# A gated recurrence feeding an MLP on one core: another hand-written order of steps, products of the state in two halves, and two 64-byte gaps in the memory map

## The chip, the core and the metric

One core of one Trainium2 chip. The metric is the device time of one execution in microseconds, the median over runs. All inputs lie in the chip's memory before the execution starts, and the output of 384 x 3072 float32 is written back to it.

## The reference, cut

```python
# q, k, v, alpha: (4, 8, 768, 48); w_in: (384, 2048); w_out: (2048, 384)
for t in range(S):
    state = alpha[:, :, t, :, None] * state + einsum('bhd,bhde->...', k[:, :, t], v[:, :, t])   # an outer product
    y[:, :, t] = einsum('bhd,bhde->bhe', q[:, :, t], state)
x = y.transpose(0, 2, 1, 3).reshape(3072, 384)
h = x @ w_in
sp = maximum(h, 0) + log1p(exp(-abs(h)))
return (h * erf(sp)) @ w_out
```

A recurrence over 768 steps for 32 heads of 48 channels (the attention part), and behind it an MLP from 384 to 2048 and back to 384, in float32 precision.

## The kernel before, in words

**Chunks.** The 768 steps are cut into 12 chunks of 64. A chunk's attention is written as matrix products: decays are accumulated by a scan (`a1`), keys and queries are scaled by them (`a2`, `a3`), `s` multiplies keys by queries (64 products, line 293), `t` transposes the keys (8 products, line 309), `u` adds the chunk to the running state T (64 products, line 326, then VectorE), `q` multiplies queries by the old state and `y` multiplies the masked scores by the values (128 products each, line 362), both into the same accumulator `py`. A chunk gives 256 tokens of x, and each chunk has its own MLP (`Moe`).

**MLP.** x is split into a high and a low part (`x_hi`, `x_lo`), the weights too (`wi_hi`, `wi_lo`, `wo_hi`, `wo_lo`), and three products hi*hi, hi*lo, lo*hi stand for one of full precision. The 2048 hidden channels of a chunk go in 4 groups of two halves: `H` multiplies by w_in (18 products of 128x256 a half, line 443), `U`, `L1`, `L2`, `G`, `Z` make the gated value on ScalarE and VectorE, and `O` splits it into `gh` and `gl` and multiplies by w_out (18 products of 128x256 a half, line 509). These are 3456 "big" products in all; the attention makes 4504 "small" ones. A product is two instructions of TensorE's stream, a weight load (PEld) and a matmul (PE).

**Weights.** They arrive as 8-byte floats in 28 pieces (`wi_0` to `wi_11`, `wo_0` to `wo_15`) and are turned into a high and a low float32 part by some six operations of ScalarE and VectorE each. The first group of H needs wi_0, wi_1 and wi_2.

**Order.** Every step is a Python generator that yields after each piece of work. `SCHED` is one long text of step names, written out by hand or by a program that is not part of the kernel; `steps()` takes the names one after another, and each name lets its step run on to its next yield (`v:` in front puts a copy on VectorE in place of ScalarE). TensorE, ScalarE, VectorE and the queue of SyncE keep exactly this order, so the text sets what each engine does next; semaphores do the waiting. Behind a `q` a memset of `token` on GpSimd is made to wait for it, and the first instruction of that chunk's `y` waits for the token.

**Memory.** `tile_pool`s are laid out one behind the other: constants and weights, then `at` (T), `xp` (x_hi and x_lo, two of each), `big` (23 buffers of 4160 bytes), `gp` (gh, gl and the output tile, two of each).

Of the kernel before, what the change touches and what calls it, by code (L numbers as in the profile page):

```python
# [30 lines left out]
la_0 a1_0 a2_0 a2_0 a2_0 la_2 a1_2 la_1 a1_1 lq_0 a3_0 wi_5 wi_5 a2_0 v:wi_5 lk_0 wi_5 a2_0 a2_1 a2_1 wi_1 wi_5 wi_0  # L31
a2_0 a2_1 wi_0 v:wi_0 lv_0 t_0 lk_1 a2_1 wi_5 wi_0 a2_1 a2_2 s_0 a2_2 s_0 s_0 y_0 a2_1 wi_2 wi_1 a2_2 wi_0 v:wi_1 wi_1
t_0 t_0 t_1 lq_1 a3_1 wi_2 v:wi_2 u_0 t_1 s_1 wi_1 wi_4 wi_4 u_0 s_1 wi_3 t_1 wi_1 v:wi_4 lv_1 wi_2 s_1 wi_2 q_1 wi_3
wi_0 wi_0 y_1 wi_7 v:wi_3 u_1 wi_2 wi_4 wi_2 wo_13 y_0 wi_1 y_0 H_0_0_0 H_0_0_1 wi_6 y_1 wi_8 wi_7 v:wi_7 wi_11 wi_4
y_1 y_1 wo_13 wi_10 wi_3 y_0 v:wo_13 wi_4 y_0 H_0_0_0 lk_2 wi_3 wi_6 wo_13 v:wi_6 wi_3 wi_7 wi_5 wi_9 H_0_0_0 wi_6
wi_4 wo_10 wi_8 wi_3 v:wi_8 H_0_0_1 H_1_0_0 H_1_0_1 H_0_0_1 U_0_0 u_1 wi_10 a2_2 H_1_1_0 wo_3 L1_0_0 H_0_1_0 H_0_1_0
y_1 wo_2 wi_9 wi_8 H_0_1_0 wi_6 wi_8 v:wi_9 H_1_1_1 H_1_0_1 lq_2 H_1_0_0 a2_2 wi_8 wo_10 v:wi_10 wi_6 wi_7 wi_7 wi_8
wo_0 wi_9 la_3 wo_3 wi_11 H_1_1_0 H_1_1_0 H_1_1_1 lv_2 v:wi_11 H_0_1_1 wi_6 v:wo_3 wi_7 H_0_2_1 a2_2 wo_13 t_2 L1_0_0
wo_13 a3_2 H_0_1_1 H_1_1_1 H_0_2_1 wi_9 H_1_0_1 H_0_1_1 H_0_2_0 wo_13 wi_9 s_2 wo_0 wi_11 wi_10 H_1_0_0 v:wo_10 v:wo_0
wo_2 wi_11 q_2 wi_9 t_2 H_0_2_0 H_1_2_0 v:wo_2 H_0_2_1 wi_10 a1_3 t_2 u_2 wo_1 wo_14 s_2 s_2 y_2 wi_11 H_0_2_0 wo_3  # L40
wi_10 wi_10 a2_3 wo_1 wo_9 v:wo_1 wo_2 wo_10 H_1_2_0 wi_11 lq_3 L1_0_0 a2_3 H_0_3_0 wo_9 H_0_3_1 u_2 v:wo_9 wo_14
v:wo_14 L2_0_0 a2_3 G_0_0 wo_10 wo_2 wo_2 wo_3 L2_0_0 H_1_2_0 lk_3 H_1_2_1 wo_14 a2_3 H_0_3_1 wo_2 H_0_3_0 a2_3 wo_14
H_1_3_0 U_0_1 y_2 y_2 y_2 a3_3 H_1_2_1 y_2 H_0_3_0 wo_5 lv_3 a2_3 L1_0_1 wo_3 wo_3 wo_6 H_0_3_1 wo_10 Z_0_0 H_1_3_1
wo_14 wo_14 wo_1 H_2_2_1 H_1_3_1 H_1_3_1 H_1_3_0 H_1_3_0 wo_6 v:wo_6 H_2_1_1 t_3 Z_0_0 H_1_2_1 wo_4 s_3 q_3 wo_5 t_3
t_3 u_3 v:wo_5 L1_0_1 O_0_0_1 L1_0_1 wo_9 s_3 s_3 wo_6 wo_1 wo_0 y_3 O_0_0_0 y_3 U_0_3 wo_5 u_3 wo_0 wo_4 O_0_0_0
wo_11 v:wo_1 L2_0_1 O_0_0_1 H_2_0_1 H_2_0_0 y_3 wo_1 H_2_1_0 y_3 wo_12 U_0_2 G_0_1 wo_9 y_3 H_2_2_0 wo_0 wo_0 H_2_0_0
v:wo_4 wo_4 L2_0_1 wo_7 wo_4 Z_0_1 L1_0_2 H_3_2_0 wo_9 L1_0_2 wo_10 H_2_2_0 H_2_2_0 wo_8 wo_6 H_2_0_0 H_2_2_1 H_3_3_1
wo_7 wo_7 H_2_0_1 L1_0_3 wo_15 Z_0_1 wo_12 wo_12 wo_7 v:wo_6 wo_4 v:wo_11 H_2_0_1 wo_7 O_0_0_0 H_3_3_1 wo_8 O_0_0_0
L1_0_2 O_0_1_0 wo_9 wo_4 L2_0_2 H_2_1_0 v:wo_8 H_3_3_1 H_3_0_0 L1_0_3 wo_5 wo_7 L1_0_3 L2_0_2 H_2_1_1 H_2_1_0 wo_6
v:wo_5 H_3_3_0 wo_7 wo_5 wo_8 wo_12 v:wo_11 wo_11 O_0_1_0 wo_8 wo_11 G_0_2 L2_0_3 O_0_0_1 H_3_0_1 H_2_2_1 lq_4 H_3_3_0  # L50
# [729 lines left out]
```

## Time and profile before

| | |
|---|---|
| median of 3 runs | 563.23 us (559.36 to 564.34) |
| the profiled execution | 559.77 us, of which the span from first to last instruction is 558.0 us |
| TensorE matmuls busy | 498.1 us (89%) |
| VectorE busy | 481.1 us (86%) |
| ScalarE busy | 474.2 us (85%) |
| mean granted clock of TensorE | 0.964 of full speed |
| moved by DMA | 43.8 MB |

How to read it: the busy time of TensorE counts every moment in which at least one product is in flight, so it does not tell how fast products follow each other. Idle time with the releaser "issue" is time in which an engine had no semaphore left to wait for in the profile and still did not start its next instruction. q8 is the DMA queue that carries TensorE's instructions.

### The profile page before, as it was taken

Reading aid. Unit: us, or ns where it says so; the run is one execution under the profiler, and the core shown is the slowest. Engines: PE = TensorE matmul, PEld = TensorE weight load, DVE = VectorE, ACT = ScalarE, POOL = GpSimd, SP = SyncE. Lnnn points to the kernel's source line nnn. Section 1 sums busy time; section 2 is a strip of 40 time slices with the busy share of each in tenths; the row PEclk is TensorE's granted clock in tenths of the full one; section 3 lists DMA queues with packets and bytes.
Section 4 is the critical chain, followed back from the end, with each engine's and each line's share of the span. In section 5 each row is a group of like instructions: output and inputs, shape, how many; then the busy total and the mean of one; then the engine's idle time right before and its main releaser. Section 6 shows DMA issues by size and latency. Waiting matters only on the chain.

```text
span 558.0 us, 17772 instructions
## 1 busy us (share of the span) xinstructions
PE 498.1 (89%) x7962; PEld 486.9 (87%) x7962; DVE 481.1 (86%) x583; ACT 474.2 (85%) x626; POOL 4.2 (1%) x25
## 2 busy tenths in 40 slices
PE   0659979799999989799799799989899998999994
PEld 0549979799999989799799799979899998999994
DVE  6858796889999998899799699988899998999892
ACT  5836996889999989799889798897899899798870
POOL 2000000000000000000000000000000000000000
PEclk9958979899999999999999799999999999999997
DMA  8874152212132141202102210221012200000001
GB/s 333 300 257 163 45 187 95 92 55 77 39 127 95 40 146 38 80 2 86 60 1 105 80 39 21 86 79 51 20 41 67 75 3 12 20 2 29 29 2 62
DMA packets 16019, 43.78 MB, mean 78 GB/s; under 512 B 1600, under 2 KB 6208, under 8 KB 15936
## 3 DMA queue, kind: packets, MB, share of 16 engines
q1 hardware_dynamic: 15936, 42.57, 21.9%
q8 instruction: 64, 1.05, 0.8%
q14 instruction: 19, 0.16, 0.1%
HBM read 37.85 MB, written 4.72 MB: 76 GB/s over the span
## 4 chain that ended last, share of the span: by engine, by line
PE 89%; issue 7%; DVE 2%; DMA 1%; POOL 0%; DVEq 0%
PE ph L443 38%; PE acc L509 37%; PE py L362 7%; PE pu L326 3%; PE pS L293 3%; PE pn L309 2%; DVE A L258 1%; DMA A<-in_alpha_dram 1%; DVE Q L281 0%; DVE K L276 0%; DVE rw L271 0%; DVE sT L300 0%; DVE o L210 0%; DVE wbuf L559 0%; DVE wbuf L555 0%
## 5 line engine op out<-in xcount | busy, mean ns | idle before, releaser
L443 PE MATMUL ph<-x_hi,wi_hi 128*128 128x256 f32 x576 | 145.5, 289 | 0.0
L443 PE MATMUL ph<-x_hi,wi_lo 128*128 128x256 f32 x576 | 144.5, 288 | 0.0
L509 PE MATMUL acc<-gh,wo_hi 128*128 128x256 f32 x576 | 139.7, 280 | 0.6 <-issue 0.6
L509 PE MATMUL acc<-gh,wo_lo 128*128 128x256 f32 x576 | 139.0, 279 | 0.0
L443 PEld LDWEIGHTS ph<-x_hi,wi_hi 128*128 128x128 f32 x576 | 112.5, 195 | 0.7 <-issue 0.3
L443 PEld LDWEIGHTS ph<-x_hi,wi_lo 128*128 128x128 f32 x576 | 112.4, 195 | 0.0
L509 PEld LDWEIGHTS acc<-gh,wo_hi 128*128 128x128 f32 x576 | 108.0, 188 | 1.1 <-issue 0.8
L509 PEld LDWEIGHTS acc<-gh,wo_lo 128*128 128x128 f32 x576 | 108.1, 188 | 0.0
L200 ACT ACTIVATE s<-s 128x1024 f32<-128x1024 f32 x96 | 100.5, 1056 | 4.3 <-DVE t L473 3.9
L443 PE MATMUL ph<-x_lo,wi_hi 128*128 128x256 f32 x576 | 82.5, 284 | 3.0 <-issue 3.0
L509 PE MATMUL acc<-gl,wo_hi 128*128 128x256 f32 x576 | 80.9, 280 | 0.0
L443 PEld LDWEIGHTS ph<-x_lo,wi_hi 128*128 128x128 f32 x576 | 74.7, 191 | 3.5 <-issue 3.2
L497 DVE TENSOR_TENSOR gl<-hs,gh 128x512 fp32r<-128x512 f32 x96 | 65.0, 685 | 12.2 <-PE acc L509 9.1
L509 PEld LDWEIGHTS acc<-gl,wo_hi 128*128 128x128 f32 x576 | 73.3, 188 | 0.2
L206 ACT ACTIVATE hs<-ph 128x512 f32<-128x512 f32 x88 | 50.6, 591 | 20.2 <-PE ph L443 20.1
L473 DVE TENSOR_TENSOR t<-s,w 128x1024 f32<-128x1024 f32 x48 | 58.1, 1218 | 1.8 <-ACT w L200 1.5
L199 ACT ACT_TABLE_LOAD x46 | 59.0, 1283 | 0.8
L484 DVE TENSOR_TENSOR s<-s,w 128x1024 f32<-128x1024 f32 x48 | 57.9, 1218 | 1.4 <-ACT s L200 1.0
L475 DVE SCALAR_TENSOR_TENSOR w<-t,w 128x1024 f32<-128x1024 f32 x48 | 58.3, 1217 | 0.2
L486 DVE SCALAR_TENSOR_TENSOR hs<-s,hs 128x1024 f32<-128x1024 f32 x48 | 58.2, 1217 | 0.1
L200 ACT ACTIVATE w<-w 128x1024 f32<-128x1024 f32 x48 | 50.4, 1055 | 0.4
L200 ACT ACTIVATE w<-s 128x1024 f32<-128x1024 f32 x48 | 50.0, 1056 | 0.3
(66 smaller groups left out, 581.6 us busy)
## 6 DMA issues: line engine op xcount, KB each, us to landing
A<-in_alpha_dram SPq DMA_DIRECT2D x12, 520.0 KB, 4.1
Q<-in_qk_dram SPq DMA_DIRECT2D x12, 512.0 KB, 3.5
wst<-in_moe_w_in_dram SPq DMA_DIRECT2D x12, 512.0 KB, 7.1
K<-in_qk_dram SPq DMA_DIRECT2D x12, 512.0 KB, 3.5
raw_v<-in_v_dram SPq DMA_DIRECT2D x12, 512.0 KB, 3.2
wst<-in_moe_w_out_dram SPq DMA_DIRECT2D x16, 384.0 KB, 3.6
out_dram<-o SPq DMA_DIRECT2D x12, 256.0 KB, 2.2
out_dram<-o SPq DMA_DIRECT2D x12, 128.0 KB, 1.7
```

The lines of the kernel that those rows point to most:

```text
L199: nc.scalar.preload_act_table_set(table)
L200: nc.scalar.activation(*args, **kw)
L206: nc.scalar.activation(out, in_, AF.Copy, scale=scale)
L293: nc.tensor.matmul(out=ps[half][i * TC : (i + 1) * TC, m * NP + pair, :], lhsT=K[rows, m, pair, i, :], rhs=Q[rows, m, pair, i, :], start=T ...
L362: nc.tensor.matmul(out=self.py[i][c0 : c0 + 32, kt, m, :], lhsT=left[r0 : r0 + rows, l0 : l0 + 32], rhs=right[r0 : r0 + rows], start=kt == ...
L443: nc.tensor.matmul(out=ph[:, u * self.TB : (u + 1) * self.TB], lhsT=wt[:, kt, fs], rhs=xt[:, kt, : self.TB], start=k == 0 and u == 0 and k ...
L473: nc.vector.tensor_tensor(out=t, in0=s, in1=w, op=ALU.mult)
L475: nc.vector.scalar_tensor_tensor(out=w, in0=t, scalar=2.0, in1=w, op0=ALU.add, op1=ALU.mult)
L484: nc.vector.tensor_tensor(out=s, in0=s, in1=w, op=ALU.mult)
L486: nc.vector.scalar_tensor_tensor(out=h, in0=s, scalar=RT2 / 2, in1=h, op0=ALU.subtract, op1=ALU.mult)
L497: nc.vector.tensor_tensor(out=gl, in0=gg, in1=gh.bitcast(F32), op=ALU.subtract)
L509: nc.tensor.matmul(out=self.acc[dm // n][:, dm % n * self.TB : (dm % n + 1) * self.TB], lhsT=wt[:, f, dm * P : (dm + 1) * P], rhs=gt[:, u ...
```

## The change

It has three parts.

1. `terms()` loops over the batch half m outside and yields after each m, so that `q` and `y` each become two pieces of 64 products; `q` now has 2 names in `SCHED` and `y` 6 (5 before).
2. `SCHED` is another text. The same 7960 products, loads and elementwise operations are issued, in another order.
3. Two tiles of 16 float32 (64 bytes a partition) that nothing uses, `shift_x` behind T and `shift_g` behind `big`. `xp` and `big` begin 64 bytes later than before, `gp` 128 bytes later.

```diff
+    def shift(name):
+        fast.enter_context(tc.tile_pool(name=name, bufs=1)).tile([P, 16], F32, name=name, tag=name)
     at = fast.enter_context(tc.tile_pool(name="at", bufs=1))
+    shift("shift_x")
     xp = fast.enter_context(tc.tile_pool(name="xp", bufs=2))
     big = fast.enter_context(tc.tile_pool(name="big", bufs=NBIG))
+    shift("shift_g")
     gp = fast.enter_context(tc.tile_pool(name="gp", bufs=2))
...
         def terms(self, old):
...
-            for kt in range(KT):
-                for w, d0 in PIECES[kt]:
-                    for m in range(M):
+            for m in range(M):
+                for kt in range(KT):
+                    for w, d0 in PIECES[kt]:
                         for part in range(2):
...
+                yield
         def q(self):
-            self.terms(True)
-            yield
+            yield from self.terms(True)
         def y(self):
...
-            self.terms(False)
-            yield
+            yield from self.terms(False)
             yield from moe.put(self.py, at0)
```

Of the order, TensorE's share is what the argument needs. Read off the two texts, with [n] for n big products in a row; `q` and `y` are 128 products before, 64 for each name after:

```
before: t_0 s_0 y_0 t_1 u_0 s_1 q_1 y_1 u_1 [150] t_2 [24] s_2 q_2 [18] u_2 y_2 [120] t_3 s_3 q_3 u_3 y_3 [390]
q_4 s_4 [36] y_4 t_4 [102] u_4 [102] s_5 t_5 [42] q_5 u_5 y_5 [162] t_6 s_6 q_6 u_6 y_6 [306] t_7 s_7 q_7 u_7 y_7 [246]
t_8 [6] s_8 q_8 u_8 y_8 [378] t_9 s_9 q_9 u_9 y_9 [162] t_10 [6] s_10 u_10 q_10 [12] y_10 [468] s_11 q_11 [6] y_11 [720]

after: t_0 s_0 u_0 y_0 y_0 t_1 s_1 q_1 q_1 [36] y_1 y_1 u_1 [84] q_2 s_2 q_2 t_2 [36] y_2 u_2 y_2 [108] q_3 t_3 [6]
s_3 u_3 q_3 [24] y_3 y_3 [372] q_4 [30] q_4 s_4 [18] t_4 y_4 y_4 [36] u_4 [96] t_5 q_5 s_5 q_5 [66] y_5 u_5 y_5 [216]
q_6 t_6 [6] s_6 q_6 [24] y_6 u_6 y_6 [300] q_7 s_7 q_7 t_7 [66] y_7 u_7 y_7 [96] q_8 t_8 [12] s_8 u_8 q_8 [18] y_8 y_8 [396]
t_9 [42] q_9 s_9 q_9 [42] y_9 u_9 y_9 [204] q_10 s_10 q_10 [18] t_10 [30] y_10 u_10 y_10 [204] q_11 s_11 q_11 [102]
y_11 y_11 [768]
```

At the start the two texts differ for the other engines too. After the change VectorE does, up to the low part of wi_2, which is the last operation that the first big product needs: a1_0, a1_1, a1_2, a3_0, three operations of a2_0, one of a2_1, one of wi_1, one of a2_1, two of s_0, u_0, one of wi_0, one of a2_1, one of wi_0, a3_1, and one each of wi_2, wi_1, wi_2, wi_0, wi_1, wi_2. The scaled x of chunk 0 follows right behind. SyncE's loads begin with la_0 la_1 la_2 lq_0 lv_0 wi_1 lk_0 wi_0 wi_2 wi_4 lk_1 lq_1; before it was la_0 la_2 la_1 lq_0 wi_5 lk_0 wi_1 wi_0 lv_0 lk_1 wi_2 lq_1. The number of switches between ScalarE's two tables is 46 in both orders. Five copies of x_hi and one of gh change between the engines: VectorE makes 3 of 24 copies of x_hi and 38 of 96 of gh, before 8 and 39.

## Rows read from the trace of the kernel before

**Rows 1.** The page: busy time, share and instructions of each engine.
```profile
PE 498.1 (89%) x7962; PEld 486.9 (87%) x7962; DVE 481.1 (86%) x583; ACT 474.2 (85%) x626; POOL 4.2 (1%) x25
```

**Rows 2.** Waits of TensorE, 0:60, 60:340, 340:550: who, for what: us, times, longest.
```profile
PE pu L326 <- issue: 4.2, 2, 2.2
PE py L362 <- issue: 3.8, 2, 3.2
...
PE py L362 <- issue: 10.3, 7, 1.9
PE pu L326 <- issue: 5.0, 3, 1.9
PE ph L443 <- issue: 3.0, 1, 3.0
PE acc L509 <- issue: 0.6, 1, 0.6
...
PE py L362 <- issue: 6.1, 5, 1.5
PE pu L326 <- issue: 1.0, 1, 1.0
```

**Rows 3.** Timeline, matmuls, chunk 6: start, us, line, tiles, xcount [idle before].
```profile
223.22 1.15 PE L362 MATMUL py<-Q,T 48*32 48x64 f32 x95
225.69 0.48 PE L362 MATMUL py<-Q,T 48*32 48x64 f32 x33 [1.32 <-issue]
226.10 1.15 PE L326 MATMUL pu<-raw_v,kn 64*64 64x48 f32 x64
227.18 0.45 PE L362 MATMUL py<-sT,raw_v 64*32 64x64 f32 x30
229.51 1.18 PE L362 MATMUL py<-sT,raw_v 64*32 64x64 f32 x98 [1.89 <-issue]
```

**Rows 4.** DMA view, instruction queue, 223:235 and then 477:537: transfers, MB, share.
```profile
q8 instruction: 4, 0.07, 2.2%
...
q8 instruction: 4, 0.07, 0.5%
```

**Rows 5.** Stretches: A:B us, busy us (xcount) of PE, PEld, DVE, ACT, POOL, clock, DMA.
```profile
60.00:340.00 280.00, 261.17 (x4515) 255.25 (x4514) 249.03 (x305) 253.96 (x348) 0.68 (x7) 0.97 0.22 74
120.00:220.00 100.00, 97.92 (x1503) 96.16 (x1502) 95.07 (x112) 95.66 (x130) 0.23 (x2) 1.00 0.23 79
79.10:84.80 5.70, 5.70 (x27) 5.70 (x28) 5.54 (x8) 4.74 (x7) 0.00 (x0) 0.50 0.58 182
105.90:108.70 2.80, 2.80 (x14) 2.80 (x14) 2.80 (x6) 2.80 (x5) 0.00 (x0) 0.51 0.57 161
316.50:320.40 3.90, 3.90 (x23) 3.85 (x19) 3.73 (x7) 2.50 (x3) 0.00 (x0) 0.52 0.42 139
```

**Rows 6.** Big products of H and O: two stretches as above; then weight loads, busy us, mean ns.
```profile
49.00:63.50 14.50, 14.50 (x125) 14.50 (x124) 9.12 (x14) 13.72 (x22) 0.00 (x0) 1.00 0.35 121
538.00:549.00 11.00, 11.00 (x96) 11.00 (x95) 8.34 (x11) 4.70 (x7) 0.00 (x0) 1.00 0.11 36
...
L443 PEld LDWEIGHTS ph<-x_hi,wi_hi 128*128 128x128 f32 x576 | 112.5, 195 | 0.7 <-issue 0.3
L509 PEld LDWEIGHTS acc<-gh,wo_hi 128*128 128x128 f32 x576 | 108.0, 188 | 1.1 <-issue 0.8
```

**Rows 7.** Timeline of the start, VectorE and TensorE.
```profile
4.50 6.76 DVE L258 TENSOR_TENSOR_SCAN A<-A,lower 128x1040 f32<-128x1040 f32 x3 [4.50 <-DMA A<-in_alpha_dram]
...
12.29 1.22 DVE L271 TENSOR_TENSOR rw<-A,r 128x1024 f32<-128x1024 f32 x1
...
21.01 1.29 DVE L300 TENSOR_TENSOR sT<-pS,maskn 128x512 f32<-128x512 f32 x2 [1.15 <-PE pS L293]
...
35.41 1.28 DVE L566 TENSOR_TENSOR wi_lo<-wbuf,wi_hi 128x512 fp32r<-128x512 f32 x2
...
44.70 0.58 PE L443 MATMUL ph<-x_hi,wi_hi 128*128 128x256 f32 x1
```

More of the change, by code (lines that the diff above doesn't have):

```diff
@@ L30 @@
 SCHED = """
[L31 to L50, printed above, removed]
@@ L126 @@
-v:O_10_3_0 O_10_3_0 O_10_2_1 O_11_1_1 O_11_1_1 O_10_3_0 L1_11_3 Z_11_2 L1_11_3 L1_11_3 L2_11_3 O_11_2_0 O_11_1_1
-O_10_3_1 G_11_3 O_10_3_0 O_11_2_0 O_10_3_1 O_11_2_0 O_10_3_1 L2_11_3 Z_11_3 O_11_2_0 O_10_3_1 O_11_2_1 O_11_2_1
-O_11_2_1 O_11_2_1 Z_11_3 v:O_11_3_0 out_10_0 v:O_11_3_1 out_10_0 O_11_3_0 O_11_3_0 O_11_3_0 out_10_1 out_10_1 O_11_3_1
+la_0 a1_0 a2_0 la_1 a1_1 a2_0 a2_0 la_2 lq_0 a2_1 lv_0 a1_2 a2_2 a2_1 a2_1 a3_0 a2_0 a2_0 wi_1 lk_0 a2_0 wi_1 t_0 wi_0
+v:wi_1 wi_2 a2_1 wi_1 t_0 t_0 wi_4 lk_1 s_0 a2_1 s_0 u_0 wi_0 v:wi_0 s_0 lq_1 u_0 wi_2 v:wi_2 wi_0 y_0 a2_1 y_0 wi_6
@@ new lines @@
+wi_4 wi_0 t_1 wi_5 a3_1 s_1 q_1 a2_2 a2_2 wi_0 wi_2 t_1 wi_6 v:wi_4 wi_1 wi_1 wi_2 wi_2 y_0 y_0 wi_5 wi_0 wi_1 wi_2
+y_0 y_0 wi_4 q_1 v:wi_5 wi_5 H_0_0_1 t_1 H_0_0_0 wi_7 wi_7 wi_3 v:wi_7 H_0_0_1 wi_3 H_0_0_0 s_1 lv_1 wo_14 v:wi_3 wi_5
+wi_5 v:wi_6 s_1 y_1 y_1 lq_2 wi_8 wi_4 wi_4 u_1 H_0_0_0 wi_3 H_0_0_1 wi_5 wi_3 wi_6 y_1 y_1 wi_9 wi_3 U_0_0 wi_4 lk_2
+y_1 wo_14 wi_3 wi_11 wo_2 H_1_0_0 wo_1 H_1_0_1 y_1 H_1_0_0 a2_2 wi_6 wi_9 wi_10 H_0_1_0 wi_8 v:wi_8 a2_2 a3_2 H_1_1_0
+wi_6 H_0_1_0 lv_2 H_1_0_0 wi_7 L1_0_0 wi_11 H_1_1_0 H_1_1_1 wi_8 L1_0_0 v:wi_9 H_1_0_1 u_1 q_2 H_1_1_0 a2_2 s_2
@@ new lines @@
+wo_0 wo_6 wo_3 v:wo_7 wo_3 wo_9 v:wo_7 wo_6 v:wo_6 H_2_0_1 H_3_3_0 L1_0_2 v:wo_4 H_2_3_1 wo_7 wo_6 H_2_0_1 wo_11
+v:wo_9 wo_7 H_3_3_1 v:wo_9 H_2_0_0 L1_0_3 Z_0_1 wo_4 v:wo_7 H_2_3_0 wo_11 wo_12 H_2_2_0 L1_0_3 O_0_0_0 wo_4 wo_7
+H_3_3_0 wo_4 L2_0_3 Z_0_1 L1_0_2 H_3_3_1 H_2_2_1 v:wo_11 H_3_3_1 G_0_3 wo_6 wo_6 O_0_0_0 H_3_2_1 L2_0_2 wo_15 L2_0_2
+wo_4 wo_4 wo_6 O_0_0_1 H_3_2_0 O_0_1_0 H_2_2_1 O_0_1_0 wo_9 wo_15 wo_11 O_0_0_1 wo_15 L2_0_3 G_0_2 H_2_2_1 H_2_2_0
+H_3_2_0 Z_0_2 O_0_1_0 wo_11 U_1_0 O_0_1_1 O_0_1_1 lk_4 H_3_0_0 la_4 wo_9 U_1_1 L1_1_1 O_0_1_0 H_3_2_1 Z_0_2 a1_4 wo_11
@@ new lines @@
+v:wo_9 Z_0_3 L1_1_0 H_2_2_0 wo_9 O_0_2_0 lq_4 H_3_1_0 Z_0_3 O_0_2_0 wo_11 H_3_2_1 O_0_1_1 L1_1_1 H_3_0_1 O_0_2_1
+O_0_1_1 L1_1_1 H_3_1_1 a2_4 O_0_2_1 O_0_2_0 L1_1_0 a2_4 H_3_1_1 H_3_2_0 O_0_2_0 a2_4 wo_12 a3_4 L2_1_1 wo_12 H_3_0_1
+H_3_0_1 H_3_1_1 L1_1_0 O_0_2_1 H_3_1_0 O_0_2_1 a2_4 q_4 wo_12 a2_4 L2_1_0 O_0_3_0 O_0_3_0 O_0_3_0 G_1_1 H_2_1_1
+H_3_0_0 H_2_1_0 O_0_3_0 O_0_3_1 a2_4 O_0_3_1 G_1_0 H_3_1_0 lv_4 q_4 s_4 U_2_0 L2_1_1 L2_1_0 s_4 s_4 U_1_2 Z_1_0
+O_0_3_1 U_1_3 H_2_1_0 L1_1_3 t_4 t_4 y_4 Z_1_0 y_4 la_5 lq_5 Z_1_1 O_1_0_0 O_1_0_0 y_4 y_4 O_0_3_1 O_1_0_0 out_0_0
@@ new lines @@
+U_6_2 H_7_1_1 L2_5_2 O_5_1_0 Z_5_3 H_8_1_1 O_5_1_0 G_5_2 Z_5_2 L1_6_1 L2_6_0 H_8_1_1 L1_6_3 O_5_1_1 O_5_1_1 Z_5_2
+O_4_3_1 L2_6_0 L1_6_1 O_4_3_0 O_4_3_1 a2_9 v:O_5_2_0 L1_6_3 L1_6_1 L2_6_1 L2_6_1 O_5_1_1 a2_9 L1_6_3 O_5_2_0 a2_9
+O_4_3_1 H_7_2_0 a2_9 O_5_2_0 O_4_3_1 H_8_1_1 H_7_0_1 O_5_2_0 O_5_2_1 a2_9 a2_9 out_4_1 out_4_1 L1_6_2 G_6_1 Z_6_1
+la_10 O_5_2_1 H_8_3_0 out_4_0 O_5_2_1 Z_6_1 H_7_2_0 G_6_0 Z_6_0 Z_6_0 O_5_3_0 H_7_0_1 out_4_0 H_7_0_0 O_5_2_1 U_7_3
+H_7_2_1 v:O_6_0_0 O_5_3_0 U_7_1 L1_6_2 H_7_0_1 lq_9 v:H_7_2_1 O_5_3_0 L1_6_2 H_7_0_0 H_7_2_0 O_5_3_1 L2_6_3 O_5_3_1
@@ new lines @@
+O_8_3_0 O_8_3_0 L1_11_0 O_9_0_1 Z_9_1 O_9_1_0 L2_11_0 v:O_8_3_1 O_8_3_0 O_9_1_0 O_9_1_0 O_8_3_1 L1_10_2 L1_10_2
+O_8_3_1 L1_10_2 O_10_0_0 Z_9_3 O_9_1_0 O_8_3_1 O_9_1_1 Z_10_1 out_8_1 out_8_1 L2_10_2 L1_11_1 L1_10_3 O_10_0_0
+O_10_0_0 L1_10_3 H_11_2_0 L2_11_1 L2_10_2 O_9_1_1 O_10_0_0 O_9_1_1 v:O_9_2_0 H_11_3_1 out_8_0 O_9_1_1 G_10_2 H_11_2_0
+v:O_10_0_1 L2_11_0 L2_11_1 out_8_0 O_10_0_1 Z_9_3 O_10_0_1 G_11_0 O_9_2_0 O_9_2_0 H_11_3_0 U_11_2 O_9_2_0 Z_11_0
+Z_11_0 O_10_0_1 O_9_2_1 O_9_2_1 O_9_2_1 L1_11_2 H_11_3_1 O_10_1_0 L1_10_3 O_10_1_0 L2_10_3 O_9_2_1 O_11_0_0 O_11_0_0
@@ L129 @@
+O_10_3_0 O_11_2_0 O_11_2_0 O_10_3_1 O_10_3_1 O_10_3_1 G_11_3 O_11_2_1 O_11_2_0 O_10_3_1 Z_11_3 O_11_2_1 Z_11_3
+v:O_11_3_1 O_11_2_1 O_11_2_1 out_10_0 out_10_0 O_11_3_0 O_11_3_0 O_11_3_0 O_11_3_0 v:out_10_1 out_10_1 O_11_3_1
 O_11_3_1 O_11_3_1 v:out_11_0 out_11_1 out_11_1 out_11_0
```

145 lines of the change are left out of this document (70 added, 75 removed).

## The prediction

> **What bounds the kernel now.** I read the page first. TensorE is busy 89% of the span, VectorE 86%, ScalarE 85% [rows 1]: three engines near their limit, TensorE first. Then the waits of TensorE. Behind the start it waits for no other engine; all 18 waits are put down to "issue", 18.9 us in 60:340 and 7.1 us in 340:550, and four more of 8.0 us lie in the start [rows 2]. They are almost all in the small products of `q`, `u` and `y`, though each of those has its operands. The timeline of chunk 6 shows the pattern [rows 3]: 95 products of q in 1.15 us, a wait, then 33 + 64 + 30 = 127 products, a wait, then the rest. 127 products are 254 instructions, and the instruction queue moved 4 transfers of 0.07 MB in all (16 KB each, 256 instructions of 64 bytes) in these 12 us; where only big products run it moves 4 in 60 us [rows 4]. So TensorE's stream comes in blocks of 128 products. From one resumption to the next it took 229.51 - 225.69 = 3.82 us [rows 3], for products that by themselves take 1.4 to 1.7 us. I read this as: the next block but one is asked for when a block is entered, and it comes some 3.8 us later. A block must hold enough work to last that long. One of big products only lasts 15 us (60 us for 4 blocks), a purely small one does not last half of it.
>
> [...]
>
> **The change part by part.** The sum starts from the profiled execution, 559.8 us. That is a low one of the three runs, 3.5 us under their median.
>
> *Waits after the start.* 26.0 us idle in 18 waits. Idle counts from the modelled end of the last product, and 95 in 1.15 us with a spacing near 0.01 us means that the last is in flight for 0.2 us. So a wait costs 0.2 more than its idle time: 26.0 + 18 x 0.2 = **29.6 us**. What is left of it in the new order I counted: counted along the old list of TensorE steps, chunk 6's waits stand at products 3537 and 3664 [rows 3]; the other waits, located the same way, lie on the same grid of 128, which slides by some 29 products over the run. I laid this grid over both lists. Before, 20 of 61 blocks hold no big product; after, 2 do, both in the start. After the start the poorest blocks of the new order hold 6 to 19 big products among 109 to 122 small ones and last 2.9 to 3.8 us (big ones at 0.118, small at 0.011 to 0.017, a transpose at 0.11), short of 3.8 by 0.9, 0.7, 0.7, 0.6, 0.6, 0.5 and less. The trace gives some head start: the wait behind big products was 1.32 us where the one behind another wait was 1.89, 0.57 less [rows 3]. Over that only 0.6 us stand out in all; I leave **1 us**. Bounds: 0, and 6 us if there is no head start.
>
> *The clock.* The three stretches cost 5.70 x 0.50 + 2.80 x 0.49 + 3.90 x 0.48 = 6.1 us [rows 5]. They follow attention runs that crawl; in 120:220, where runs were shorter, the clock stayed at 1.00. I take **5 us** back; bounds 0 and 6.1.
>
> *The start.* Before, the first big product starts at 44.70 [rows 7], behind all of chunks 0 and 1. After, 36 of them stand between q_1 and y_1. They need the low part of wi_2, the 23rd VectorE operation of the new order: 3 scans 6.8, 6 + 2 operations of a2 and a3 at 1.22, two of s_0 1.3 with 1.15 of waiting for their products, u_0 put at 1.0, 9 of weights at 0.64, from 4.5 on: 4.5 + 6.8 + 9.8 + 2.4 + 1.0 + 5.8 = 30.3 us [rows 7]. With 36 products at the lower clock (5.70/27 = 0.211 us each, [rows 5]) 7.6 us, y_1 1.5, u_1 1.1 [rows 3] and half a us of wait, chunks 0 and 1 and 36 big products are done at 41.0. Before, the same stood at 44.7 + 12 x 0.211 + 24 x 0.118 = 50.1. That gives **9 us**. Lower bound: only the waits go, 8.0 less the 2.1 + 1.2 + 1.2 that the three poor blocks of the new start (1.7, 2.6, 2.6 us long) lack to 3.8: 3.5. Upper bound: at the full clock, 36 x 0.118 and no wait, 13.
>
> *More changes of kind.* The new order has 28 runs of small products behind the first big one, the old one 19. At each return to big products one weight load, 0.19 us [rows 6], has nothing to hide behind: 9 x 0.19 = **1.7 us** more.
>
> *VectorE.* In 60:340 it works 249.0 of 280 us [rows 5]. Of these 280, 18.9 + 12 x 0.2 = 21.3 us of waits and 6.1 of clock go: 252.6 are left, and VectorE would have to work 98.6% of them. The best 100 us that the trace shows are 95.07% [rows 5]. At 96% the stretch takes 259.4: TensorE waits **7 us** for VectorE (in gl, x_lo or freed buffers) which it didn't before. Bounds: 0, and 18 at 92%. The five x_hi copies that leave VectorE take only 2 us from it. ScalarE (254.0) stands beside it and is counted in the same 7.
>
> *Two gaps.* x lies a multiple of 128 bytes from the weights now, gh and gl 64 bytes off one. After, both lie 64 off. The trace has both kinds: a stretch of w us meets w/spacing + 2.4 products (0.28 us in flight), so H runs at 14.5/122.6 = 0.1183 and O at 11/93.6 = 0.1175 us, with loads of 195 and 188 ns [rows 6]. If only that distance counts, 1728 products of H gain 0.8 ns: **1.4 us**. Bounds: no row shows the new addresses; half-clock products at 0.211 put the floor at 0.106 at full clock, 12 ns under today's, and I allow as much upward. [...]
>
> *At nothing:* the second token of each `q` (in the new order other products lie between the last `q` and the first `y` of a chunk, and the wait before was 0.2 us in one place), the turned loops in `terms` (same products, same inner order), the moved loads (SyncE's queue only issues; over 60:340 the DMA engines are busy 0.22 of the time, and up to 0.58 in the stretches [rows 5]). If a load comes late, its chunk's `a2` is late next, and VectorE behind it: part of the 7.
>
> Sum: 559.8 - 29.6 + 1 - 5 - 9 + 1.7 + 7 - 1.4 = 524.5; with some of the old runs' spread above the profiled one, **525 us**, against 563.2 (a ratio of 0.93).
>
> **The rivals.**
>
> *VectorE takes over.* What TensorE gains it waits away, because VectorE can't go above some 92% with this many hand-overs. For it: 98.6% wanted; against: 95% in 120:220, and no wait of TensorE for VectorE after the start even there. 18 us in place of 7, and as much again of the start's 9 lost in part: 536 to 542. Chance 0.14.
>
> *The grid lies otherwise.* If the boundaries fall elsewhere in the new stream (semaphore instructions shift them), full blocks fit into its runs of 192 to 200 small products, of which there are about 13; half of them would wait 2 us: 538. Against: the semaphore instructions that make the grid slide are nearly the same in both, and the slide over the whole run was 29 products. Chance 0.05.
>
> *The waits aren't those of blocks.* Then 29.6 us stay and so does the clock's share, and more runs cost 1.7: 552 with the start's gain, 561 without. For it speaks only that the wait is inferred. [...] Chance 0.03.
>
> *The gaps matter much, downward.* With the spacing 5 ns nearer to its floor, 3456 x 5 ns = 17 us more go, of which VectorE gives back half: 515, and 505 with 10 ns. Chance 0.05.
>
> *Slower.* The same place the other way: if the new distance between x, gh and the weights makes a load collide, each ns of spacing costs 3.5 us. It ends above the old time from 44/3.456 = 12 to 13 ns on, at 0.130 us a product: 570. For it: loads differ by 7 ns between two distances; against: the spacing differs by 0.8. Chance 0.03.
>
> **How the numbers follow.** The forecast (waits gone, VectorE keeps up within 10 us) has 0.70. The range: down to 524.5 - 7 (VectorE never late) - 4 (start) - 2 = 511; up to 524.5 + 11 (VectorE at 92%) + 4 = 540, which takes in the first two rivals. Outside lie the gaps' extremes and no gain, and half of the tails: under 2 in 10. About 1% is what a measurement of this kernel can tell from no change. Faster by more: forecast, two middle rivals, the gaps downward, and half of the third: 0.95. Within: 0.02. Slower: 0.03.
>
> **What would show it.** In the profile after: "issue" waits of TensorE after 45 us down from 26 to a few us; the first line-443 product near 31 us; no run of small products with a wait in it; the clock at 1.00 throughout after some 45 us; new waits of TensorE on VectorE or ScalarE, some 7 us, mostly before 250 us; weight loads of H at 188 ns like O's; VectorE and ScalarE at 90% and more of the span. Wrong would be: "issue" waits of 10 us or more after the start (the block rule), TensorE waiting more than 15 us on VectorE (the rival), or spacing outside 0.117 to 0.119 (the gaps).

## The result and the profile after

The changed kernel takes 510.94 us (median of 4 runs, 509.78 to 511.87) against 563.79 us (559.36 to 564.67) before: a ratio of 0.908, interval 0.902 to 0.913. The profiled execution of after took 511.07 us, its span is 509.4 us, and it is the one that is compared below with the 559.77 us of before. The forecast was 525, with a range of 511 to 540: the direction and most of the steps came, and 14 us more, which is the low end of the range. Every median here is that of the fast executions, those within 1.5% of their kernel's fastest.

The page of after: busy time, share and instructions of each engine, the answer to [rows 1].

```profile
PE 479.0 (94%) x7962; PEld 468.1 (92%) x7962; DVE 477.0 (94%) x580; ACT 471.8 (93%) x629; POOL 5.1 (1%) x36
```

The three engines did what they did before (VectorE 481.1 then, 477.0 now) in 48.6 us less, so all three shares rose to 93 or 94%.

Waits of TensorE after, 0:60 and then 60:340, as in [rows 2]; 340:550 has none.

```profile
PE pn L317 <- DVE K L284: 15.9, 1, 15.9
PE py L370 <- issue: 3.7, 3, 2.2
PE ph L450 <- DVE sT L308: 1.2, 1, 1.2
...
PE pu L334 <- issue: 0.6, 1, 0.6
PE acc L516 <- ACT gh L214: 0.4, 1, 0.4
PE ph L450 <- issue: 0.4, 1, 0.4
```

Where 18 waits on "issue" took 26.0 us behind the start, two take 1.0. No wait for VectorE stands there at all, and the one for ScalarE (gh) is 0.4 us.

Stretches of after: A:B us, busy us (xcount) of PE, PEld, DVE, ACT, POOL, clock, DMA. The first answers the first of [rows 5], the second is the start; the others hold big products only.

```profile
60.00:340.00 280.00, 278.46 (x4915) 271.71 (x4899) 273.85 (x333) 276.94 (x378) 1.24 (x14) 1.00 0.25 80
29.00:42.00 13.00, 9.55 (x312) 8.86 (x306) 8.73 (x16) 8.01 (x16) 0.18 (x2) 0.87 0.81 290
105.00:129.00 24.00, 24.00 (x206) 24.00 (x205) 23.80 (x30) 23.75 (x36) 0.00 (x0) 1.00 0.18 67
210.00:241.00 31.00, 31.00 (x276) 31.00 (x275) 30.89 (x37) 30.58 (x39) 0.00 (x0) 1.00 0.18 60
484.00:497.00 13.00, 13.00 (x117) 13.00 (x116) 12.51 (x16) 10.24 (x12) 0.00 (x0) 1.00 0.03 11
```

Two things to see. In 60:340 VectorE works 97.8% and ScalarE 98.9% of the time, and TensorE still isn't kept waiting. And the big products stand closer together: with the prediction's working (2.4 products in flight), 484:497 gives 13/114.6 = 0.1134 us, where the last stretch of before gave 0.1175 [rows 6]. Inside after there are two spacings: 31/273.6 = 0.1133 in 210:241, and 24/203.6 = 0.1179 in 105:129, which is that of before.

The start of after, timeline of TensorE (start, us, line, tiles, xcount [idle before]), the answer to [rows 7].

```profile
27.21 0.33 PE L370 MATMUL py<-Q,T 48*32 48x64 f32 x13
28.52 1.74 PE L370 MATMUL py<-Q,T 48*32 48x64 f32 x115 [0.98 <-issue]
30.19 0.58 PE L450 MATMUL ph<-x_hi,wi_hi 128*128 128x256 f32 x1
...
32.28 0.33 PE L450 MATMUL ph<-x_hi,wi_lo 128*128 128x256 f32 x1
32.44 0.28 PE L450 MATMUL ph<-x_hi,wi_hi 128*128 128x256 f32 x1
32.56 0.28 PE L450 MATMUL ph<-x_hi,wi_lo 128*128 128x256 f32 x1
34.04 0.28 PE L450 MATMUL ph<-x_hi,wi_hi 128*128 128x256 f32 x1 [1.20 <-DVE sT L308]
...
36.87 1.28 PE L370 MATMUL py<-sT,raw_v 64*32 64x64 f32 x104
40.40 0.43 PE L370 MATMUL py<-sT,raw_v 64*32 64x64 f32 x24 [2.25 <-issue]
40.76 1.15 PE L334 MATMUL pu<-raw_v,kn 64*64 64x48 f32 x64
41.84 0.38 PE L450 MATMUL ph<-x_hi,wi_hi 128*128 128x256 f32 x1
```

The first big product starts at 30.19, and chunks 0 and 1 with 36 big products are done at 41.84.

### The profile page after: what moved, and what is told of

The parts are those of the page before. It is cut to its first block, busy times and chain, and to the rows that moved or that the text cites. A ratio compares the mean times of both kernels' runs of the same rounds, so it can differ in the third digit from the quotient of the medians.

```text
span 509.4 us, 17790 instructions
## 1 busy us (share of the span) xinstructions
PE 479.0 (94%) x7962; PEld 468.1 (92%) x7962; DVE 477.0 (94%) x580; ACT 471.8 (93%) x629; POOL 5.1 (1%) x36
## 3 DMA queue, kind: packets, MB, share of 16 engines
q8 instruction: 64, 1.05, 0.9%
## 4 chain that ended last, share of the span: by engine, by line
PE 80%; ACT 10%; DVE 5%; issue 3%; DMA 1%; DVEq 0%; ACTq 0%
PE ph L450 35%; PE acc L516 33%; PE py L370 6%; ACT s L208 3%; ACT w L208 3%; PE pu L334 3%; PE pS L301 2%; PE pn L317 2%; ACT hs L214 1%; ACT L207 1%; ACT gh L214 1%; DVE A L266 1%; DMA A<-in_alpha_dram 1%; DVE wbuf L566 0%; DVE wbuf L562 0%
## 5 line engine op out<-in xcount | busy, mean ns | idle before, releaser
L450 PE MATMUL ph<-x_hi,wi_hi 128*128 128x256 f32 x576 | 138.3, 281 | 1.6 <-DVE sT L308 1.2
L516 PE MATMUL acc<-gh,wo_hi 128*128 128x256 f32 x576 | 137.3, 280 | 0.4 <-ACT gh L214 0.4
L450 PE MATMUL ph<-x_hi,wi_lo 128*128 128x256 f32 x576 | 137.4, 280 | 0.0
L516 PE MATMUL acc<-gh,wo_lo 128*128 128x256 f32 x576 | 136.0, 278 | 0.0
L450 PEld LDWEIGHTS ph<-x_hi,wi_lo 128*128 128x128 f32 x576 | 109.3, 190 | 1.7 <-issue 1.7
L450 PEld LDWEIGHTS ph<-x_hi,wi_hi 128*128 128x128 f32 x576 | 109.2, 190 | 0.7 <-issue 0.2
L450 PE MATMUL ph<-x_lo,wi_hi 128*128 128x256 f32 x576 | 79.8, 279 | 0.0
L450 PEld LDWEIGHTS ph<-x_lo,wi_hi 128*128 128x128 f32 x576 | 72.2, 188 | 0.3
L516 PEld LDWEIGHTS acc<-gl,wo_hi 128*128 128x128 f32 x576 | 71.9, 188 | 0.5
L208 ACT ACTIVATE s<-hs 128x1024 f32<-128x1024 f32 x48 | 49.9, 1058 | 2.7 <-DVE w L482 2.1
```

The source lines that it names most:

```text
L208: nc.scalar.activation(*args, **kw)
L450: nc.tensor.matmul(out=ph[:, u * self.TB : (u + 1) * self.TB], lhsT=wt[:, kt, fs], rhs=xt[:, kt, : self.TB], start=k == 0 and u == 0 and k ...
L516: nc.tensor.matmul(out=self.acc[dm // n][:, dm % n * self.TB : (dm % n + 1) * self.TB], lhsT=wt[:, f, dm * P : (dm + 1) * P], rhs=gt[:, u ...
```

## The experiments

The kernels with one time beside them ran once; of these the argument rests on the spacing and the waits, and not on differences of 1 or 2 us between their times. In every run the spacing of big products is the mean time from the start of one to the start of the next, both of H or both of O, at full clock and under 0.140 us apart: some 1,540 to 1,600 pairs of each kind in each kernel. The rows shown beside it are stretches that hold big products only.

**The order alone and the gaps alone.** The gaps are taken apart from the rest of the change. The first kernel is after without the gaps, so the new order with `q` and `y` in halves (these two were not taken apart from each other):

```diff
-    shift("shift_x")
...
-    shift("shift_g")
```

> The changed kernel without the two gaps: new order and halved products alone. Gap theory (the distance between moving and stationary operand sets how fast big products follow each other): spacing goes back to 0.117 to 0.119 us everywhere, no stretch at 0.113, and the time is some 8 to 11 us above the changed kernel, 519 to 522 us. Order theory (the spacing is set by what stands between the runs of big products): the two spacings 0.113 and 0.118 stay and the time is within 2 us of 511. Both: no wait put down to issue above 1 us after the start.

Measured: 520.39 us (519.71 to 522.56), a ratio of 0.924 to before (0.917 to 0.930). The spacing is 0.1183 for H and 0.1177 for O, that of before to 0.1 ns. Stretches of this kernel, one of H and one of O:

```profile
87.00:102.00 15.00, 15.00 (x129) 15.00 (x128) 14.96 (x31) 14.98 (x27) 0.00 (x0) 1.00 0.43 134
492.00:506.00 14.00, 14.00 (x122) 14.00 (x121) 12.63 (x17) 10.50 (x12) 0.00 (x0) 1.00 0.03 11
```

Its weight loads of H, from the page (busy us, mean ns of one, idle before):

```profile
L448 PEld LDWEIGHTS ph<-x_hi,wi_hi 128*128 128x128 f32 x576 | 108.3, 188 | 0.5
```

So the order gives 43.4 us of the 52.9, and the gaps 9.45 us behind it. The loads of H take 188 ns here, at the same distance at which they took 195 in before [rows 6]. The 195 is a mean over stretches at a granted clock of 1.00 and of 0.50 to 0.52 [rows 5]: at full clock the loads of H in before take 188 ns too, like those of O, and 66 of them, in the stretches at the lower clock, take 328. Two loads of before, one to either side of the clock's rise (start, us):

```profile
46.79 0.33 PEld L443 LDWEIGHTS ph<-x_hi,wi_hi 128*128 128x128 f32 x1
...
47.22 0.19 PEld L443 LDWEIGHTS ph<-x_hi,wi_hi 128*128 128x128 f32 x1
```

So the 7 ns say nothing of the distance.

The second is the kernel before with both gaps, the old order unchanged:

```diff
+    shift("shift_x")
     xp = fast.enter_context(tc.tile_pool(name="xp", bufs=2))
...
+    shift("shift_g")
     gp = fast.enter_context(tc.tile_pool(name="gp", bufs=2))
```

> The kernel before with the two gaps alone. Gap theory: stretches with 0.1133 us between big products appear in the old order, about half to three quarters of them, and the time falls by 4 to 10 us under the kernel before, 553 to 559 where that one has 563. Order theory: spacing stays at 0.118, time within 2 us of before. Both: the 18 waits put down to issue after the start stay, 26 us give or take 3.

Measured: 549.79 us (548.37 to 553.09), a ratio of 0.976 (0.967 to 0.986): more gain than expected. The spacing fell to 0.1142 (H) and 0.1138 (O), 4.0 ns under before, which over 3456 products is 13.8 us; 19 waits on "issue" of 28.0 us stay, 2 us more than before. The same two stretches as in [rows 6], as this kernel has them:

```profile
48.00:62.00 14.00, 14.00 (x126) 14.00 (x126) 9.46 (x14) 11.72 (x18) 0.00 (x0) 1.00 0.43 142
522.00:539.00 17.00, 17.00 (x152) 17.00 (x151) 15.09 (x20) 10.76 (x13) 0.00 (x0) 1.00 0.07 25
```

| us | no gaps | both gaps |
|---|---|---|
| old order | 563.79 | 549.79 |
| new order | 520.39 | 510.94 |

Both parts act by themselves. Their gains don't quite add: the gaps give 14.0 us in the old order and 9.45 in the new. Of the 4.6 us between, 2.8 are the spacing, which in the mean of both kinds is 0.8 ns shorter in the old order than in after; the rest is not accounted for.

**Are the waits those of blocks?** The instruction stream is shifted against the grid of blocks of 128 products: in chunk 0, `s` issues some of its products twice, with the same values to the same place, so that all that follows moves by 44 or by 112 products. The rest of after stands as it is. (Each call of the loop is two products.)

```diff
+            for z in range(22 if self.first else 0):   # 56 for 112 products
+                m, pair, par, i = z // 32 % 2, z // 4 % 4, z // 2 % 2, z % 2
+                half = par ^ i
...
+                nc.tensor.matmul(
+                    out=ps[half][i * TC : (i + 1) * TC, m * NP + pair, :],
+                    lhsT=K[rows, m, pair, i, :], rhs=Q[rows, m, pair, i, :], start=True, stop=True,
+                )
```

> The changed kernel, in which the scores of chunk 0 issue 44 of their 64 products a second time (the same values into the same place), so that every later product sits 44 places further in the instruction stream. Nothing else moves. Block theory (a block of 128 products must last some 3.5 to 3.8 us, or TensorE waits for the next one): the grid now falls onto the runs of small products; some 16 waits of 1 to 2 us put down to issue appear after the start, 15 to 25 us in all, and the time is 525 to 537 us. Rival (a wait comes from the length of a run of small products in itself): 0.5 to 1.5 us more than the changed kernel, 511 to 513 us, and no new wait.

> As the run with 44 products issued again, but 112 of them, so that the grid comes back to within 16 products of where it was. Block theory: 0 to 2 us of waits put down to issue after the start, the time 513 to 516 us although more products were added than in the run with 44. Rival (added work or run length): more than the run with 44 costs, in proportion, 1 to 3 us above the changed kernel.

Measured: 540.20 us with 44, 3 us above what the theory of blocks gave for it, and 516.23 with 112. In both the start is later than in after: chunks 0 and 1 and 36 big products are done at 46.2 and 46.9 in place of 41.8. With 112 that is 5.1 of the 5.3 us that it lies above after. Waits of TensorE with 44, 60:340 and then 340:550:

```profile
PE py L378 <- issue: 13.8, 10, 2.3
PE pS L301 <- issue: 0.3, 1, 0.3
...
PE py L378 <- issue: 7.7, 5, 2.8
```

A stretch of the same kernel, right behind one of the waits:

```profile
60.30:64.30 4.00, 4.00 (x44) 3.90 (x44) 4.00 (x5) 2.64 (x6) 0.09 (x1) 0.58 0.35 103
```

Waits of TensorE with 112, 60:340; on "issue" there is none, and 340:550 has no wait:

```profile
PE acc L524 <- ACT gh L214: 1.1, 1, 1.1
PE ph L458 <- ACT hs L214: 0.7, 2, 0.6
```

With 44 products more the waits are back, 17 of 23.1 us behind 45 us, in an order that waited 1.0 us; 68 products further they are gone (one of 1.6 us is left, at 45.6). Only a grid in the stream does that: the same steps in the same order wait or don't by where a boundary falls in them. The instruction queue says the same: each of the 17 waits, and each of the 22 of before, ended 1.2 to 1.6 us after a transfer of q8 had landed. In before there are 64 of these transfers, of 16 KB each, for 15,924 weight loads and matmuls: 249 to a transfer, where a grid of 128 products makes 256. The clock came down too, three times for 3.4 us behind 45 us, each time behind one of these waits, and the row shows one of them (0.58 over the stretch). So here the boundaries cost 23.1 us where the products were small, and 1.0 us in after.

**What is it in the gaps?** The prediction counted the distance of the moving operand (x, gh, gl) from the weights modulo 128 bytes. With the first gap alone, x lies 192 bytes from the weights (modulo 512) and the gated values 128:

```diff
-    shift("shift_g")
```

> The changed kernel with the first gap alone: x lies 192 bytes (modulo 512) from the weights as in the changed kernel, gh and gl 128 bytes, which is where x lay before. Theory 1 (each kind of product is set by its own distance): O falls back to some 0.1183 us with no stretch at 0.113, H keeps a mean near 0.115; time 515 to 518 us. Theory 2 (only 64 off a multiple of 128 counts, as the prediction had it): the same for O. Theory 3 (the faster spacing needs both, since it is handed on from one product to the next): neither has a stretch at 0.113, 519 to 522 us.

```profile
87.00:100.00 13.00, 13.00 (x117) 13.00 (x116) 12.94 (x26) 12.98 (x23) 0.00 (x0) 1.00 0.38 126
490.00:504.00 14.00, 14.00 (x120) 14.00 (x120) 12.50 (x16) 10.68 (x13) 0.00 (x0) 1.00 0.03 11
```

Measured: 518.11 us. H (first row) has 117 products in 13 us, O 120 in 14: 0.1149 and 0.1188 in the mean of all pairs, as the first two theories had it. Each kind goes by its own distance, and in the mean 64 and 192 are not the same place: O had 0.1177 at 64.

Then other distances, as gaps of other sizes. Both operands at 160, 224 and 256; at 320 and 448; at 384 and 512 (x first):

```diff
-    def shift(name):
-        fast.enter_context(tc.tile_pool(name=name, bufs=1)).tile([P, 16], F32, name=name, tag=name)
+    def shift(name, n):
+        fast.enter_context(tc.tile_pool(name=name, bufs=1)).tile([P, n], F32, name=name, tag=name)
...
+    shift("shift_x", 8)     # 24, 32, 48, 64
...
+    shift("shift_g", 16)    # 16, 16, 48, 48
```

> The changed kernel with a first gap of 32 bytes in place of 64 and the second of 64: x, gh and gl all lie 160 bytes from the weights. Theory of the prediction (two kinds, a multiple of 128 or 64 off one) says nothing here. If the spacing goes step by step with the distance, it lies between the 0.118 at 128 and the 0.115 at 192: a mean of 0.116 to 0.117, time 512 to 517 us. If 64-byte lines decide, 160 counts as 128: no stretch at 0.113, 519 to 522 us.

> The changed kernel with a first gap of 96 bytes and the second of 64: x, gh and gl all lie 224 bytes from the weights. If 64-byte lines decide, 224 counts as 192: both spacings, 0.113 and 0.118, mean near 0.115, 508 to 513 us. If the spacing goes on falling with the distance, a mean below 0.114 and 505 to 509 us.

> The changed kernel with a first gap of 128 bytes and the second of 64: x, gh and gl all lie 256 bytes from the weights. The prediction's reading (a multiple of 128 is the worse kind) expects what x had at 128: 0.1183 us, no stretch at 0.113, 519 to 522 us. If the distance modulo 256 or 512 counts, 256 is a place not seen yet, and 0.106 (half of the spacing at the lower clock) to 0.124 is open.

> The changed kernel with gaps of 192 and 192 bytes: x lies 320 bytes (modulo 512) from the weights, gh and gl 448. Each kind of product has gone by its own distance so far, so one run reads two. If the distance counts modulo 256: H at 320 goes as O did at 64 in the kernel before, 0.1177 us, and O at 448 as at 192, a mean of 0.115 with stretches at 0.113. If it counts modulo 128: both as at 64 or 192, not told apart. If modulo 512 or more: places not seen yet, 0.106 to 0.124. Time 514 to 518 us in the first case.

> The changed kernel with gaps of 256 and 192 bytes: x lies 384 bytes (modulo 512) from the weights, gh and gl 0. If the distance counts modulo 256: H at 384 goes as at 128, 0.1184 us, and O at 0 as at 256, 0.1199; time 521 to 524 us. If modulo 512 or more: places not seen yet.

Stretches with x at 320 (H) and the gated values at 448 (O):

```profile
92.00:105.00 13.00, 13.00 (x113) 13.00 (x112) 12.96 (x28) 12.98 (x21) 0.00 (x0) 1.00 0.50 154
489.00:503.00 14.00, 14.00 (x126) 14.00 (x125) 13.44 (x18) 10.80 (x14) 0.00 (x0) 1.00 0.03 11
```

With both at 256, a stretch of O:

```profile
497.00:511.00 14.00, 14.00 (x119) 14.00 (x118) 12.25 (x16) 10.52 (x12) 0.00 (x0) 1.00 0.03 11
```

Measured: 521.76, 521.34, 525.00, 516.68 and 523.66 us. 448 gives O the close spacing of 192 (126 products in 14 us, 119 at 256), and 320 gives H that of 64 (0.1176 us, where O had 0.1177): of these places the distance counts modulo 256 bytes. Of the expectations for 160 and 224 neither a smooth fall nor lines of 64 bytes is left: 160 would fit the lines, 224 with 0.1183 fits neither. At 256 the spacing is 1.6 ns above what the prediction's reading gives. A last one asked how wide the good place is, with x at 176 and the gated values at 208 (gaps of 32 and 96 bytes, and the tiles of x, gh and gl 64 columns wider, of which the first four are skipped):

```diff
-            self.x = tuple(self.pl.xp.tile([P, KT, XB], F32R, name=n, tag=n) for n in ("x_hi", "x_lo"))
+            self.x = tuple(
+                self.pl.xp.tile([P, KT * XB + 64], F32R, name=n, tag=n)[:, 4 : 4 + KT * XB].rearrange("p (k t) -> p k t", k=KT)
+                for n in ("x_hi", "x_lo")
+            )
...
-            gh = self.pl.gp.tile([P, 512], F32R, name="gh", tag="gh")
+            gh = self.pl.gp.tile([P, 576], F32R, name="gh", tag="gh")[:, 4:516]
```

> After with other gaps (32 and 96 bytes) and with the tiles of x and of the gated values 64 columns wider, read from their fourth column on, so that the distance of x from its weights is 176 bytes and that of the gated values 208 bytes (both beside a multiple of 512): 16 bytes to either side of the 192 of after. All products are those of after. If only a distance of 192 itself is good, both spacings are those of 160 and 224, 0.1179 to 0.1183 us, and the time is 520 to 523 us. If the spacing goes over smoothly between the measured places, they lie between, 0.1155 to 0.1175, and the time is 513 to 519. If 192 is not the best place, one of the two is under 0.1144 and the time of its half is less than in after.

Measured: 524.13 us, with 0.1191 and 0.1187 us: 16 bytes beside 192 nothing of its gain is left, and the spacing is even 0.3 to 1.1 ns above that of 160 and 224, which nobody expected. Part of the time is its start, where the clock stayed low for 10.2 us (3.4 in after).

| distance modulo 256 | H | O | from the kernels |
|---|---|---|---|
| 0 | 0.1199 | 0.1192, 0.1199 | both at 256; gated values at 512 |
| 64 | 0.1176 | 0.1177 | x at 320; before |
| 128 | 0.1184, 0.1187 | 0.1188 | before, x at 384; first gap alone |
| 160 | 0.1181 | 0.1178 | both |
| 176 | 0.1191 | | |
| 192 | 0.1142 to 0.1152 | 0.1138 to 0.1145 | after, gaps in the old order, first gap alone, 448 |
| 208 | | 0.1187 | |
| 224 | 0.1183 | 0.1183 | both |

The means hide what single pairs show. In after, at 192, nearly every pair is either at 0.113 to 0.114 or at 0.117 to 0.119 us. At 64 the same two occur, but nearly all pairs are in the second: in before 39 of 1,599 pairs of O were under 0.115. The kernel without gaps ran its last 34 pairs of O, at 64, at 0.1133. So 64 and 192 differ in which of the two is taken, and not in the two themselves. With both at 256 nearly all pairs are at 0.120; at 128, 160, 176, 208 and 224 they are spread, most of them between 0.112 and 0.125.

**Do the other engines make the spacing?** At the very end of each kernel stand stretches in which VectorE, ScalarE and GpSimd do nothing and no DMA moves. One with both at 256, one of the kernel without gaps, one of the last kernel below (both at 192):

```profile
513.40:514.60 1.20, 1.20 (x13) 1.20 (x12) 0.00 (x0) 0.00 (x0) 0.00 (x0) 1.00 0.00 0
508.10:509.20 1.10, 1.10 (x12) 1.10 (x12) 0.00 (x0) 0.00 (x0) 0.00 (x0) 1.00 0.00 0
499.50:500.60 1.10, 1.10 (x12) 1.10 (x11) 0.00 (x0) 0.00 (x0) 0.00 (x0) 1.00 0.00 0
```

From start to start the products there are 0.120, 0.1133 and 0.1133 us apart. In after, at 192, and in before, at 64, a stretch of this kind has 0.118. So the two spacings and the 0.120 all occur without the work of another engine, and its being idle doesn't choose between them.

**The distance, or the place?** In all these kernels the weights stood still, so the place of the moving operand by itself would explain the table as well. The last kernel puts 64 unused bytes ahead of the weights, so that they and all behind them move together:

```diff
+    const.tile([P, 16], F32, name="ahead")
     wi_hi = const.tile([P, KT, FF], F32R, name="wi_hi")
```

> After with 64 unused bytes ahead of the weights, so that the weights and all that lies behind them (T, x, the big buffers, the gated values) move by 64 bytes together. The distances of x and of the gated values from their weights stay 192 beside a multiple of 256. So far the weights had never moved, so the distance and the place of the moving operand by itself could not be told apart. If the distance is what counts, the spacing stays at 0.1144 to 0.1152 us and the time at 510 to 513 us. If the place of the moving operand counts, x and the gated values now lie where a distance of 256 had put them: 0.1192 to 0.1199 us and 523 to 526 us. If the place of the weights counts for itself too, the spacing is another that neither says.

```profile
87.00:102.00 15.00, 15.00 (x135) 15.00 (x134) 14.82 (x31) 14.98 (x26) 0.00 (x0) 1.00 0.43 134
484.00:497.00 13.00, 13.00 (x117) 13.00 (x116) 12.51 (x16) 10.46 (x12) 0.00 (x0) 1.00 0.03 11
```

Measured: 511.39 us (510.73 to 512.28), a ratio of 0.911 (0.905 to 0.917), with 0.1145 and 0.1143 us. 135 products in 15 us of H, where the kernel without gaps had 129: the distance counts, and not the place of x or of the weights by themselves.

## Why the prediction was right or wrong

The terms of its sum, against the two profiled executions:

| term | forecast, us | measured, us |
|---|---|---|
| waits behind the start | -28.6 | -28.2 |
| clock | -5 | -6.1 |
| start | -9 | -8.3 |
| changes of kind | +1.7 | +3.5 |
| VectorE | +7 | +0.6 |
| gaps | -1.4 | -9.5 |
| behind the last big product | 0 | -1.0 |
| sum from 559.8 | 524.5 | 510.8 (the profiled 511.1) |

The gaps' 9.5 is from the medians of the kernels without and with them; their profiled executions differ by 8.8. Behind the last big product 7.8 us passed before and 6.8 after, for which the forecast had no term.

**The range: met by luck in part.** Its low end, 511, was made of VectorE never late, a better start and 2 us more (by its own terms 511.5); more from the gaps was left outside as an extreme. The 510.94 came of the first and of the gaps, and not of the start.

**Waits: right.** 1.0 us of idle in two waits, 1.4 with 0.2 each for what is in flight, where 1 was left over. The grid that was counted along the old list and laid over the new one held for the whole stream, and the shifts by 44 and 112 products showed that it is the grid. One detail was read wrongly. "The next block but one is asked for when a block is entered": behind the start of before the transfer of q8 that follows a wait begins 1.0 to 1.7 us after the wait's end, and where two waits follow each other the second ends after that same transfer has landed. So it is the next block that is fetched then. The "256 instructions of 64 bytes" are an estimate: the 1.05 MB of q8 over the 15,924 loads and matmuls of before are 66 bytes each, with whatever else the stream holds.

**Clock: right.** From 32.4 us on after runs at 1.00 up to its last 3 us; the three stretches of [rows 5] and their 6.1 us are gone. That they follow from the waits was only argued from where they stood. The kernel with 44 products more brought both back together, but three low stretches stand there against 17 waits; and the last kernel, with 64 bytes ahead of the weights, had one (80.4 to 83.9) though its waits on "issue" behind 45 us sum to 1.3 us. So a low stretch can follow a short wait, and most waits are followed by none; what decides is open.

**Start: right in its sum, by errors that cancel.** VectorE's chain was worked out to 30.3, and the first big product came at 30.19; but the chain ended at 29.63, and the product started when TensorE was through with q_1, which a wait of 0.98 had held up. That the two times agree is luck. Then 26 of the first 36 big products did not run at the lower clock (26 x 0.093 = 2.4 us less than forecast), and the waits took 0.98 + 1.20 + 2.25 = 4.4 us where half a us was put in. All three are waits for blocks. The profile puts the second down to VectorE, but the operation that it names was done at 32.4, 1.6 us before the product started; the wait stands 115 + 12 = 127 products behind the first and 128 ahead of the third, and ended 1.3 us after a transfer of q8 had landed. What failed is the 3.8 us that a block was said to need: from one of these waits' ends to the next it took 5.5 and 6.4 us here, and blocks with 12 and 24 big products, which lasted 4.3 and 4.1 us, were too short. The transfers of q8 began 3.3 and 3.8 us after a wait had ended, in place of 1.0 to 1.7. Why they began late is open; the DMA engines were busy 0.81 of the time in 29:42.

**Changes of kind: sized at half.** The step took one weight load for each return to big products. From start to start, the first small product came 0.195 us behind the last big one (28 times; before 0.175, 19 times) and the first big one 0.129 us behind the last small one (28 times; before 0.125, 19 times): 9.07 us in place of 5.71, of which the 9 big products' own spacing, 1.1, is no loss. Left: 2.3. And the new order, with `q` and `y` in halves, makes 38 changes between kinds of small products, at 0.15 us each, in place of 29: 1.2 more, for which the forecast had nothing.

**VectorE: the mechanism fell.** "At 96% the stretch takes 259.4: TensorE waits 7 us for VectorE" was worked out from the best 100 us that the trace showed, 95.07%. This was no ceiling of VectorE. Waits of VectorE in 60:340, kernel before (for what: us, times, longest):

```profile
DVE x_hi L208 <- PE py L362: 8.3, 3, 4.5
...
DVE x_lo L406 <- PE ph L443: 3.6, 1, 3.6
DVE sT L300 <- PE pS L293: 2.8, 3, 1.8
DVE T L340 <- PE pu L326: 2.8, 3, 1.4
...
DVE gl L497 <- PE acc L509: 1.5, 2, 1.2
...
DVE gh L208 <- PE acc L509: 0.6, 1, 0.6
```

19.6 of its 31 us of idle time were waits for TensorE. TensorE itself stood idle on "issue" in 3.3 us of them; in the others it was at work on something that came earlier in its order. In after VectorE waits for TensorE 0.4 us in 60:340 and works 97.8% of the time; TensorE waits for neither of the two but 0.4 us for ScalarE, 0.6 with what is in flight. The order has a part in this beside the waits: with 44 products more the waits on "issue" are back (14.0 us in 60:340), and VectorE waits for TensorE 6.2 us there. In 105:129 it works 99.2%, and ScalarE 99.0%, without a wait of TensorE. What VectorE waits for stands in none of the rows that the prediction went by. Without the gaps the forecast was 525.9, and the kernel without them took 520.39: the 5.5 us between are mostly this term, less what the changes of kind took.

**Gaps: the mechanism was found, its size and its rule weren't.** "If only that distance counts, 1728 products of H gain 0.8 ns" took the distance modulo 128, by which the 64 of before's gated values and the 192 of after are the same place. In the mean they are not: modulo 256 the place 192 had no row in before, and there both H and O have 3.2 ns less than before (0.1181 to 0.1149 us in the mean of both). The bound had allowed 12 ns; the value was taken from the nearest row, and the nearest row was of another place. The 7 ns between the loads of H and O, in which the prediction saw a sign of it, are the lower clock's and not the distance's. In the stretches with the other engines idle the spacing is 0.120 at 0 and 0.1133 at 192, so it isn't a wait for one of them; the gaps are worth 9.45 us, and 14 us lie between after and both operands at 256 (510.94 and 525.00).

**The rivals.** *VectorE takes over* (536 to 542): no, 0.4 us of waiting for ScalarE is all that stands there. *The grid lies otherwise* (538): no. It is what the kernel with 44 products more is, and that took 540. *The waits aren't those of blocks* (552 or 561): no, by the two shifts and by the transfers of q8. *The gaps matter much, downward* (515 at 5 ns, VectorE giving back half): this is what came on top of the forecast, with 3.2 ns. Of the 11.1 us that these make over 3456 products 9.45 came, so at most 1.7 were given back, and not half. *Slower* by the gaps (570): no; the worst place found is 1.5 to 2.2 ns above before's spacing.

## What to carry to other kernels

An idle share of an engine that is not the bound is no reserve or ceiling until its own waits have been read: of VectorE's 31 us of idle time in 60:340, 19.6 were waits for TensorE, and it went from 249.0 to 273.85 of 280 us when TensorE waited less. Small products in long runs were paid here by the block of 128 products, so big ones belong into each block, and a stream that just fitted stopped fitting when 44 products were put in ahead of it (waits of 23.1 us in place of 1.0). Where thousands of like products run back to back, try the distance of the moving operand from the weights in steps of 64 bytes; two unused tiles were all that it took for 9.45 us, and a row of one place told nothing of another: at 176 and 208, 16 bytes beside the good one, nothing of the gain was left (0.1191 and 0.1187 us, against 0.1152 and 0.1145).
